# The last group's output in token order, four right-side buffers, and parts spread over fourteen steps

## The chip, the cores and the metric

One Trainium2 chip; the kernel runs on one of its cores. The metric is device time in microseconds (us), the median of several executions. Names of engines: PE is TensorE's matmul, PEld its weight load, DVE is VectorE, ACT is ScalarE, POOL is GpSimd, SP is SyncE, which only issues DMAs. SPq and ACTq are the DMA issues on the queues of SP and ACT.

## What is computed

An attention with decay (retention) over 4 batches, 8 heads, 768 positions and 64 columns gives 3072 tokens of 512 columns. Two feed-forward layers follow, each 512 to 2048 to 512, everything in 32-bit floats:

```python
x = attention(q, k, v)                  # 3072 x 512
h = x @ w_in;  x = (h * cos(h)) @ w_out
h = x @ w2_in
g = np.where(h >= 1, h, np.where(h <= -1, 0.0, (h + 1) ** 2 / 4))
out = g @ w2_out                        # 3072 x 512
```

## The kernel before

**Number format.** Each matmul operand is split into a high part (fp32r, a rounding copy made by ScalarE, line 139) and a low part (the difference, made by GpSimd at line 142 or 1002, or by VectorE). A product of two operands takes three matmuls: high by high, low by high, high by low. One matmul has 128 x 128 stationary values and 512 moving columns.

**Order of the work.** The attention fills the first steps. The first layer has 96 `steps`: a step is one chunk of 128 hidden columns for one of six blocks of 512 tokens. Steps 0 to 47 take the first eight chunks for all blocks, steps 48 to 95 the other eight, and add the first half's sums when a block is finished. Step i runs `first(i)` (12 matmuls, line 681), `second(i - 3)` (12 matmuls, line 768) and `act(i)`: rounding copy on ScalarE (line 719), high and low part of the step before, `evacuate` (line 779) of a finished block's four accumulators, cosine, then `fill` (a list of extra work), then one advance of the `Conveyor`, which converts the second layer's weights. Engines work each through their own instructions in this program order.

**Weights of the second layer.** `Convert` decodes pairs of chunks; `combine` forms four sums of half chunks (line 267), and `part` writes high and low parts of each piece and queues stores to `wp` (sent by SP, line 296). A pair has four pieces, three of 512 and one of 256 columns. The last pair is started in steps 83 and 84 and its pieces are made in step 89.

**Second layer (`Products`).** It pairs blocks (three pairs p = 0, 1, 2) and pairs of hidden chunks (8), which gives 24 groups g. Each group uses a scheme with seven products in place of eight, named 11, t1, 21, t2, 22, t3, t4. The right sides are the tokens (sums and differences of quarters), the left sides are weights. Group g has seven sections; in each, PE does one product of group g (6 matmuls, line 961) and one output of group g - 1 (6 matmuls, line 977), which VectorE adds to one of four running sums (`acc`, line 1035). Between them ScalarE and VectorE evaluate the ramp and square (lines 1005, 1006, 1009, 1012, 1109, 1105, 1015) and `high` and `low` make the operands of the outputs. Operands live in a ring of eight pairs of buffers (`pairs`).

The order in which a right side's seven parts are made is `TURN`: t2, t1, t3, t4, 11, 21, 22. For p = 0 `make(0)` and `make(1)` do that in the fills of steps 80 to 95. `make(0)` places its differences in buffers that later take high parts, so that each high copy overwrites what the part made just before it was read from:

```python
at = dict(zip(TURN[:4] + ("12",), TURN[1:4] + ("11", "21")))
x.update({q: place(at[q], "h", F32) for q in at})
```

For p = 1 and 2 `remake` does it in the groups of the pair before, one `tick` per section: 11, 21, 22 of the first half, then t2, t1, t3, t4, then the same seven of the second half (11', ...). Each part's high copy goes to `xhi` (two buffers), and two stores to DRAM (`xb`, line 925) follow, the high part's in the next section.

**The end.** Group 24 has no products, only group 23's outputs. VectorE does `t4`'s difference and low parts there. The last four sums are added in halves (line 1031), and `final` transposes each with 8 PE transposes (line 1077), copies the results out of PSUM (lines 1084, 1086) into token order, and stores 256 KB per token tile (line 1091).

Of the kernel before, what the change touches and what calls it, by code (L numbers as in the profile page):

```python
# [11 lines left out]
F32 = mybir.dt.float32  # L12
# [28 lines left out]
def tile_retention_mlp_mlp(  # L41
# [42 lines left out]
        for m, j, a in [(0, j, a) for j in range(NH, NF) for a in range(2)] + order2[:READY]  # L84
# [5 lines left out]
             for g in range(NH)] for a in range(2)]  # L90

# [81 lines left out]
    class Convert:  # L173
# [72 lines left out]
        def combine(self):  # L246
# [22 lines left out]
        def part(self, n):  # L269

            to = wp_d[self.a][self.j // 2][n]
# [8 lines left out]
            stores.append((to[:, 0, :], hi[:, :wide[n]].bitcast(F32)))  # L280
# [508 lines left out]
    class Products:  # L789
# [7 lines left out]
        def __init__(self):  # L797
            self.w, self.x, self.f, self.g = {}, {}, {}, {}
            self.spare, self.ready = [], []
            self.done, self.turned, self.out = {}, {}, {}  # L800
            self.rows, self.finals = [], []
# [3 lines left out]
            self.pairs = [("wi", n) for n in range(NH + NP + 1, NF)] + [("g", 0)] * 3  # L805
# [17 lines left out]
        def load(self, a, g, n):  # L823
# [7 lines left out]
            self.w[a, g, n] = slot, t  # L831

# [72 lines left out]
        def remake(self, p):  # L905
# [12 lines left out]
            def parts(c, q):  # L918
                hi = self.tmp.tile([P, TB], F32R, tag="xhi", name="xhi", bufs=2)
# [16 lines left out]
            return fs  # L936

# [80 lines left out]
        def add(self):  # L1018
            if not self.pending:
                return  # L1020
            g, q, y, fine = self.pending.pop(0)
# [7 lines left out]
            elif fine and final:  # L1029
                for e in range(2):  # L1030
                    nc.vector.tensor_tensor(out=a[:, e, :], in0=y[:, e, :], in1=a[:, e, :], op=ALU.add)
                self.finals.append((a, p, h, n))
                return
            else:
                nc.vector.tensor_tensor(out=a, in0=y, in1=a, op=ALU.add)  # L1035
# [31 lines left out]
        def final(self):  # L1067

            if not self.finals:
                return  # L1070
            a, p, h, n = self.finals.pop(0)
            z = self.z[2 * self.nz:2 * self.nz + 2]
            self.nz = 1 - self.nz
            z = [t[:, o:o + 2 * P] for t in z for o in (0, 2 * P)]
            for e in range(2):
                for i in range(NP):
                    nc.tensor.transpose(z[i][:, e * P:(e + 1) * P], a[:, e, i * P:(i + 1) * P], self.eye)
            if h == 0:
                self.out[n] = self.big()
            for i in range(NP):  # L1080
                o = self.out[n][:, i, :].rearrange("p (k c b) -> p c k b", k=4, c=4)[:, 2 * h:2 * h + 2]
                src = z[i].rearrange("p (e k b) -> p e k b", k=4, e=2)
                if i < 2:
                    nc.vector.tensor_copy(out=o, in_=src)
                else:
                    nc.scalar.activation(out=o, in_=src, func=AF.Copy)
            if h == 0:
                return
            for i in range(NP):
                t0 = (i * NC + 2 * p + n) * C  # L1090
                (nc.sync, nc.scalar)[i // 2].dma_start(out=out[t0:t0 + C, :], in_=self.out[n][:, i, :])

        def group(self, g, banks, ends):


            live, prev = g < self.NG, g - 1
            fine = prev == self.NG - 1
# [21 lines left out]
            def outputs(q, to, begin):  # L1119
# [3 lines left out]
                if prev >= 0:  # L1123
                    self.output(prev, q, to, begin)
                    self.pending.append((prev, q, to, fine))

            def done(n, m):
                if prev >= 0:
                    self.release(1, prev, n)
                    self.load(1, g, m)  # L1130

            o = self.old
            if live:
                a = bank(banks[0])
                self.product(g, "11", a, True)
# [4 lines left out]
            if live:  # L1140
                s1 = copy(a)
            if o:
# [3 lines left out]
                fast = nc.vector if fine else nc.gpsimd  # L1146
                fast.tensor_tensor(out=t4, in0=o["r21"], in1=self.f[prev, "t2"], op=ALU.subtract)
# [4 lines left out]
            if prev >= 0:  # L1152
                self.load(1, g, 0)

            if live:
                b = bank(banks[1])
                self.product(g, "t1", b, True)
# [7 lines left out]
            if live:  # L1165
                s5 = copy(b)
# [3 lines left out]
            if live:  # L1170
                tick()

            if live:
                c = bank(banks[2])
                self.product(g, "21", c, True)
                self.release(0, g, 0)
                self.load(0, g + 1, 1)
            self.add()
            if o:
                self.low(prev, "21")  # L1180
                self.low(prev, "t4", fast)
            if live:
                plus(c, c, s1)
                r11 = self.take(g, "11")
                self.ramp(r11, c)
# [3 lines left out]
            if live:  # L1189
                tick()  # L1190

            if live:
                self.product(g, "t2", a, False)
                self.release(0, g, 1)
                self.load(0, g + 1, 2)
            self.add()
            if live:
                s6 = copy(a)
                self.square(r11)
                self.larger(r11, r11, c)  # L1200
            outputs("22", y1, False)
            self.turn_out("21")
            if live:
                tick()

            if live:
                self.product(g, "22", b, False)
            self.add()
            if live:
                self.high(g, "11")  # L1210
# [488 lines left out]
```

## Time and profile before

| what | value |
|---|---|
| median of 3 runs | 1102.06 us (1097.68 to 1102.06) |
| the profiled execution: time | 1098.7 us |
| the profiled execution: span | 1096.9 us |
| PE busy | 1070.3 us |
| DVE, POOL, ACT busy | 804.3, 614.4, 603.7 us |
| DMA | 279.95 MB, 255 GB/s |

The span runs from the first to the last instruction of the profiled execution; its time is 1.8 us more. Matmuls are pipelined: of several in a row each shows about 0.39 us, and one begins every 0.227 us. A row of the timeline has start, duration, engine, line and operation, output and inputs, shape and count, and in brackets the engine's idle time before it with what ended it.

### The profile page before, as it was taken

The numbers are of one execution on the slowest core, as the hardware profiler recorded it, in microseconds if no ns is written. First come the engines' busy times: TensorE is split into PE (matmuls) and PEld (weight loads), VectorE is DVE, ScalarE is ACT, GpSimd is POOL, SyncE is SP. The second block draws the span as 40 slices with busy tenths as digits, with TensorE's granted clock in tenths as the row PEclk, the third lists the DMA queues.
The fourth block names the chain that finished last, engine by engine and source line by source line (L and its number), as shares of the span: only waits on it lengthen the run. The fifth ranks groups of instructions, "written<-read, shape, count | busy, mean of one in ns | idle before, by whom it ended". The sixth has DMA issues, their size and how long they took to land.

```text
span 1096.9 us, 17870 instructions
## 1 busy us (share of the span) xinstructions
PE 1070.3 (98%) x6286; PEld 868.2 (79%) x6286; DVE 804.3 (73%) x1101; ACT 603.7 (55%) x1078; POOL 614.4 (56%) x525
## 2 busy tenths in 40 slices
PE   8999999999999999999999999999999899999996
PEld 5677788888888888888887888787888688888884
DVE  5778878877667447869774578678887677978776
ACT  3454334433355445546465567677677676666662
POOL 3834212221146368878998248787368785564642
PEclk9999999999999999999999999999999999999999
DMA  9588389895667599989978677889598899576542
GB/s 340 173 295 277 110 241 307 271 322 172 214 212 260 194 298 323 337 305 310 302 253 273 245 238 254 296 289 388 170 293 259 268 320 360 175 249 204 179 143 87
DMA packets 139897, 279.95 MB, mean 255 GB/s; under 512 B 15520, under 2 KB 41760, under 8 KB 139808
## 3 DMA queue, kind: packets, MB, share of 16 engines
q1 hardware_dynamic: 124256, 250.49, 69.3%
q10 hardware_dynamic: 15552, 28.32, 7.5%
q8 instruction: 50, 0.82, 0.3%
q14 instruction: 39, 0.32, 0.1%
HBM read 195.39 MB, written 83.36 MB: 254 GB/s over the span
## 4 chain that ended last, share of the span: by engine, by line
PE 83%; DMA 6%; DVE 5%; POOL 2%; issue 2%; ACT 1%; SPq 0%; DVEq 0%; ACTq 0%; POOLq 0%
PE b L768 22%; PE b L681 21%; PE b L961 17%; PE y L977 17%; PE b L580 2%; PE b L487 1%; DVE big L1043 1%; DMA xb2t20h<-xhi 1%; DMA qk<-in_qk 1%; PE b L498 1%; DMA xb1t20h<-xhi 1%; DMA wp<-whi 1%; DMA xl<-xTl 1%; DMA xb1t21h<-xhi 1%; DMA xb2t21h<-xhi 1%
## 5 line engine op out<-in xcount | busy, mean ns | idle before, releaser
L719 ACT ACTIVATE r<-b 128x512 int32<-128x512 f32 x96 | 57.1, 595 | 188.6 <-PE b L681 140.0
L724 DVE SCALAR_TENSOR_TENSOR r<-b,r 128x512 f32<-128x512 f32 x96 | 66.0, 688 | 114.7 <-ACT r L719 110.6
L230 POOL TENSOR_TENSOR cf<-cf,cs 128x512 int32<-128x512 int32 x42 | 54.4, 1295 | 147.1 <-DVE cf L221 98.3
L1035 DVE TENSOR_TENSOR xh<-y,xh 128x1024 f32<-128x1024 f32 x88 | 107.0, 1220 | 27.0 <-PE y L977 25.9
L1113 POOL TENSOR_TENSOR ft<-r,f 128x512 f32<-128x512 f32 x24 | 31.2, 1299 | 123.2 <-PE y L977 92.0
L768 PE MATMUL b<-gh,wo 128*128 128x512 f32 x384 | 98.2, 390 | 1.6 <-DVE o L779 1.6
L977 PE MATMUL y<-wi,wo 128*128 128x512 f32 x360 | 93.8, 395 | 5.5 <-ACT xhi L139 3.0
L681 PE MATMUL b<-xh,wi 128*128 128x512 f32 x384 | 94.8, 389 | 0.0
L1035 DVE TENSOR_TENSOR xl<-y,xl 128x1024 f32<-128x1024 f32 x64 | 77.9, 1216 | 13.7 <-PE y L977 13.7
L961 PE MATMUL b<-wih,wi 128*128 128x512 f32 x320 | 87.1, 390 | 0.4 <-DVE b L1105 0.4
L977 PE MATMUL y<-gh,wo 128*128 128x512 f32 x272 | 85.1, 395 | 2.3 <-DVE xh L1035 2.3
L768 PEld LDWEIGHTS b<-gh,wo 128*128 128x128 f32 x384 | 71.8, 188 | 17.5 <-ACT r L730 2.0
L977 PEld LDWEIGHTS y<-wi,wo 128*128 128x128 f32 x360 | 67.7, 190 | 22.2 <-ACT xhi L139 4.2
L681 PEld LDWEIGHTS b<-xh,wi 128*128 128x128 f32 x384 | 72.1, 188 | 14.9
L737 ACT ACTIVATE gh<-b 128x512 fp32r<-128x512 f32 x96 | 57.1, 595 | 38.0 <-DVE b L733 37.5
L768 PE MATMUL b<-gh,woh 128*128 128x512 f32 x192 | 77.4, 408 | 0.5 <-ACT woh L139 0.5
L681 PE MATMUL b<-xh,wih 128*128 128x512 f32 x192 | 75.4, 395 | 1.6 <-ACT wih L139 0.9
L681 PE MATMUL b<-xh,wil 128*128 128x512 f32 x192 | 74.3, 390 | 0.0
L768 PE MATMUL b<-gh,wol 128*128 128x512 f32 x192 | 74.0, 391 | 0.0
L1002 POOL TENSOR_TENSOR gl<-ft,gh 128x512 fp32r<-128x512 f32 x56 | 71.7, 1298 | 1.3 <-ACT gh L139 1.3
L961 PEld LDWEIGHTS b<-wih,wi 128*128 128x128 f32 x320 | 59.9, 188 | 13.6 <-DVE b L1105 1.3
L733 DVE TENSOR_TENSOR b<-b,r 128x512 f32<-128x512 f32 x96 | 66.6, 693 | 2.6 <-ACT r L730 0.3
(173 smaller groups left out, 2770.3 us busy)
## 6 DMA issues: line engine op xcount, KB each, us to landing
wi<-wp SPq DMA_DIRECT2D x66, 512.0 KB, 4.7
wo<-wp SPq DMA_DIRECT2D x66, 512.0 KB, 5.1
raw<-in_w SPq DMA_DIRECT2D x64, 512.0 KB, 6.0
wp<-whi SPq DMA_DIRECT2D x48, 256.0 KB, 3.9
wp<-s SPq DMA_DIRECT2D x32, 256.0 KB, 3.7
w<-cf ACTq DMA_DIRECT2D x26, 256.0 KB, 5.4
xTh<-xh ACTq DMA_DIRECT2D x24, 256.0 KB, 5.7
xTl<-xl ACTq DMA_DIRECT2D x24, 256.0 KB, 5.9
```

Source lines behind the costliest of these rows:

```text
L230: nc.gpsimd.tensor_tensor(out=f, in0=f, in1=self.s, op=ALU.add)
L681: nc.tensor.matmul(out=h, lhsT=w[:, c * P:(c + 1) * P], rhs=x[:, c, :], start=(i == 0), stop=(i == len(terms) - 1),)
L719: nc.scalar.activation(out=self.r.bitcast(I32), in_=self.h, func=AF.Identity, scale=INV_2PI, bias=0.25)
L724: nc.vector.scalar_tensor_tensor(out=self.r, in0=self.h, scalar=INV_2PI, in1=self.r.bitcast(I32), op0=ALU.mult, op1=ALU.subtract,)
L733: nc.vector.tensor_tensor(out=self.h, in0=self.h, in1=self.r, op=ALU.mult)
L737: nc.scalar.activation(out=self.gh, in_=self.h, func=AF.Copy)
L768: nc.tensor.matmul(out=acc[k, b][e], lhsT=w[:, s], rhs=g, start=(begin and i == 0), stop=(last and i == 2),)
L961: nc.tensor.matmul(out=to, lhsT=w[:, c * P:(c + 1) * P], rhs=x, start=begin and n == 0, stop=n == len(terms) - 1, skip_group_check=not begin,)
L977: nc.tensor.matmul(out=to[:, e, :], lhsT=w[:, e * P:(e + 1) * P], rhs=a, start=begin and m == 0, stop=m == 2, skip_group_check=not begin,)
L1002: eng.tensor_tensor(out=lo, in0=self.f.pop((g, q)), in1=hi.bitcast(F32), op=ALU.subtract)
L1035: nc.vector.tensor_tensor(out=a, in0=y, in1=a, op=ALU.add)
L1113: nc.gpsimd.tensor_tensor(out=o, in0=x, in1=z, op=ALU.subtract)
```

## The change

Three things are changed.

1. Group 23 makes no differences t1, t2, t3, t4; it keeps the four plain operands 11, 12, 21, 22, and there is no group 24. `close` runs behind it. It transposes the four sums of the groups up to 22 (`turned`, 8 PE transposes each time), copies them into token order on ScalarE, and multiplies the plain operands with plain weights (`load_plain`) so that the product is in token order already (`tile`: two halves, four tiles, 6 matmuls each). VectorE adds a tile's product to the transposed sum, and the tile is stored at once, by SP and ACT in turn. For the plain weights the last weight pair gets a fifth piece of 256 columns, `wx`.
2. `xhi` has four buffers, as two tiles of two halves. The second tile takes the place of one pair of the operand ring, which has seven pairs after.
3. `make(0)` puts its eleven fills at steps 80 + 0, 1, 3, 4, 5, 6, 8, 9, 10, 12, 13 in place of 80 + 0 to 8 with the last three in one step.

```diff
             if self.a:
                 a12, a21 = a21, a12
                 self.pieces[0] = [(a11, 0), (a12, h)]
+                if self.j == NF - 1:
+                    self.pieces[4] = [(a21, 0)]
...
                 self.part(3)
                 self.part(0)
+                if 4 in self.pieces:
+                    self.part(4)
...
-            self.pairs = [("wi", n) for n in range(NH + NP + 1, NF)] + [("g", 0)] * 3
+            self.pairs = [("wi", n) for n in range(NH + NP + 1, NF - 1)] + [("g", 0)] * 3
+            self.highs, self.turns = [], 1
...
+        def load_plain(self, n):
+            slot = self.slots[1].pop(0)
+            t = wpool[1].tile([P, 2, TB], F32R, tag=f"{slot[0]}{slot[1]}", name=f"{slot[0]}{slot[1]}")
+            h = TB // 2
+            first, *_, fourth = wp_d[1][NH - 1]
+            for o, d in ((0, first[:, :, n * h:(n + 1) * h]), (h, fourth if n else wx_d)):
+                nc.sync.dma_start(out=t[:, :, o:o + h].bitcast(F32), in_=d)
+            self.plain[n] = t[:, 0, :], t[:, 1, :]
...
             def parts(c, q):
-                hi = self.tmp.tile([P, TB], F32R, tag="xhi", name="xhi", bufs=2)
+                hi = self.next_high()
...
+        def next_high(self):
+            if not self.highs:
+                n = self.turns = 1 - self.turns
+                pool, tag = (wpool[1], f"wi{NF - 1}") if n else (self.tmp, "xhi")
+                t = pool.tile([P, 2, TB], F32R, tag=tag, name="xhi")
+                self.highs = [t[:, 0, :], t[:, 1, :]]
+            return self.highs.pop(0)
...
+        def close(self, banks):
...
+            def turned(n, i):
+                z = self.ps.tile([P, 2, TB], F32, tag=f"y{(g + 1 + i // 2) % 2}", name="z")
+                for m in range(2):
+                    for c in range(NP):
+                        a = self.acc["12"[c // 2] + "12"[n]]
+                        nc.tensor.transpose(
+                            z[:, m, c * P:(c + 1) * P], a[:, c % 2, (i + m) * P:(i + m + 1) * P], self.eye
+                        )
...
+            def half(n, i, k):
+                if k == 0:
+                    ys[i] = bank(banks[(2, 1, 3, 0)[i]])
+                (wh, wl), (gh, gl) = self.plain[k], self.g[g, names[n][k]][1]
+                for m, (a, w) in enumerate(((gh, wh), (gh, wl), (gl, wh))):
+                    nc.tensor.matmul(
+                        out=ys[i], lhsT=a[:, i * P:(i + 1) * P], rhs=w,
+                        start=k == m == 0, stop=k == 1 and m == 2,
+                    )
...
+                    t0 = (i * NC + 2 * p + n) * C
+                    (nc.sync, nc.scalar)[i % 2].dma_start(out=out[t0:t0 + C, :], in_=o)
+
+            self.add()
+            r21, h21 = self.old["r21"], self.old["h21"]
+            self.square(r21)
+            self.larger(h21, r21, h21)
+            self.f[g, "21"] = h21
+            turned(1, 0)
+            self.high(g, "21")
+            self.low(g, "21", nc.vector)
+            tile(1, 0, 1)
+            turned(1, 2)
+            tile(1, 2)
+            turned(0, 0)
+            tile(1, 3)
+            tile(0, 0)
+            turned(0, 2)
+            for i in range(1, NP):
+                tile(0, i)
...
+            if end:
+                self.f[g, "12"] = r12
+                self.high(g, "12")
+            else:
                 t1 = self.take(g, "t1")
                 minus(t1, r12, r11)
...
-                    for n, f in enumerate(fast.make(0)):
-                        ready.setdefault(i + min(n, NH), []).append(f)
+                    for n, f in zip((0, 1, 3, 4, 5, 6, 8, 9, 10, 12, 13), fast.make(0)):
+                        ready.setdefault(i + n, []).append(f)
                     for n, f in zip((0, 2, 3, 3, 3, 4, 4, 5, 5, 6, 7), fast.make(1, stage)):
                         ready.setdefault(i + NH + n, []).append(f)
```

## Rows read from the trace of the kernel before

**Rows 1.** The page: busy time; costliest groups (count | busy us, mean ns | idle before)

```profile
PE 1070.3 (98%) x6286; PEld 868.2 (79%) x6286; DVE 804.3 (73%) x1101; ACT 603.7 (55%) x1078; POOL 614.4 (56%) x525
...
L733 DVE TENSOR_TENSOR b<-b,r 128x512 f32<-128x512 f32 x96 | 66.6, 693 | 2.6 <-ACT r L730 0.3
```

**Rows 2.** What PE waited for: us in total, times, longest

```profile
PE y L977 <- ACT xhi L139: 3.0, 1, 3.0
...
PE y L977 <- POOL wi L1002: 1.7, 3, 0.7
...
PE b L768 <- DVE o L779: 1.6, 1, 1.6
```

**Rows 3.** Timeline of PE at the end

```profile
1069.76 2.88 PE L977 MATMUL y<-wi,wo 128*128 128x512 f32 x12
...
1077.19 0.71 PE L977 MATMUL y<-gh,wo 128*128 128x512 f32 x2 [2.30 <-DVE xh L1035]
```

**Rows 4.** A window: us, busy us and instructions by engine, granted clock, DMA share, GB/s

```profile
1077.20:1083.00 5.80, 5.80 (x18) 4.57 (x19) 3.98 (x5) 0.00 (x0) 0.47 (x1) 0.71 0.01 3
```

**Rows 5.** The chain that ended last: start, us, what

```profile
847.44 8.86 DMA xb2t20h<-xhi
...
1064.48 1.36 PE y L977 x6
...
1085.44 1.08 PE b L1077 x8
```

**Rows 6.** Timeline of ACT in groups 23 and 24

```profile
1056.18 0.63 ACT L139 ACTIVATE wi<-ft 128x512 fp32r<-128x512 f32 x1
...
1071.76 0.63 ACT L1009 ACTIVATE f<-f 128x512 f32<-128x512 f32 x1
...
1091.94 0.82 ACTq L1091 DMA_DIRECT2D out<-big  x2
```

**Rows 7.** DMA issues of the last 17 us: KB each, median us to landing

```profile
out<-big ACTq DMA_DIRECT2D x4, 256.0 KB, 3.0
```

**Rows 8.** What ACT waited for, the `xhi` copies: us, times, longest

```profile
ACT xhi L139 <- DMA xb2t20h<-xhi: 5.8, 1, 5.8
...
ACT xhi L139 <- DMA xb1t20h<-xhi: 2.9, 1, 2.9
...
ACT xhi L139 <- DMA xb1t21h<-xhi: 2.6, 1, 2.6
...
ACT xhi L139 <- DMA xb2t21h<-xhi: 2.2, 1, 2.2
```

**Rows 9.** Timeline of PE behind two of these waits

```profile
700.98 0.70 PE L977 MATMUL y<-wi,wo 128*128 128x512 f32 x2
...
702.43 1.19 PE L977 MATMUL y<-wi,wo 128*128 128x512 f32 x4 [0.74 <-POOL wi L1002]
...
859.49 1.16 PE L977 MATMUL y<-wi,wo 128*128 128x512 f32 x2 [3.03 <-ACT xhi L139]
...
860.90 2.08 PE L977 MATMUL y<-wi,wo 128*128 128x512 f32 x4 [0.26 <-POOL wi L1002]
```

**Rows 10.** Timeline of ACT, the last instruction before the longest of them

```profile
849.93 0.63 ACT L1006 ACTIVATE r<-r 128x512 f32<-128x512 f32 x1
```

**Rows 11.** Timeline of PE in step 91

```profile
580.48 2.43 PE L768 MATMUL b<-gh,wo 128*128 128x512 f32 x8 [1.61 <-DVE o L779]
```

**Rows 12.** Timeline of ACT, steps 87 and 90

```profile
567.50 0.63 ACT L139 ACTIVATE woh<-wih 128x512 fp32r<-128x512 f32 x1 [1.42 <-POOL wol L142]
...
577.84 0.58 ACT L719 ACTIVATE r<-b 128x512 int32<-128x512 f32 x1
```

**Rows 13.** Timeline of POOL, steps 87 and 88

```profile
568.67 1.31 POOL L142 TENSOR_TENSOR wol<-wih,woh 128x512 fp32r<-128x512 f32 x1
...
572.87 2.56 POOL L142 TENSOR_TENSOR s<-s,whi 128x512 fp32r<-128x512 f32 x2
...
577.32 2.54 POOL L142 TENSOR_TENSOR wil<-wil,wih 128x512 fp32r<-128x512 f32 x2
```

More of the change, by code (lines that the diff above doesn't have):

```diff
@@ L799, in __init__ @@
             self.spare, self.ready = [], []
-            self.done, self.turned, self.out = {}, {}, {}
-            self.rows, self.finals = [], []
+            self.done, self.turned, self.plain = {}, {}, {}
+            self.rows = []
             self.queue = [[], []]
@@ L1028, in add @@
                 nc.vector.tensor_copy(out=a, in_=y)
[L1029 to L1033, printed above, removed]
             else:
@@ L1152, in group @@
             if prev >= 0:
[L1153 to L1157, printed above, removed]
+                load(0)
+            b = bank(banks[1])
+            self.product(g, "t1", b, True)
             self.add()
@@ L1169, in group @@
             self.turn_out("22")
[L1170 to L1177, printed above, removed]
+            tick()
+            c = bank(banks[2])
+            self.product(g, "21", c, True)
+            self.release(0, g, 0)
+            self.load(0, g + 1, 1)
             self.add()
@@ L1180, in group @@
                 self.low(prev, "21")
[L1181 to L1185, printed above, removed]
+                self.low(prev, "t4")
+            plus(c, c, s1)
+            r11 = self.take(g, "11")
+            self.ramp(r11, c)
             outputs("t2", y0, False)
@@ L1188, in group @@
             done(1, 1)
[L1189 to L1195, printed above, removed]
+            tick()
+            self.product(g, "t2", a, False)
+            self.release(0, g, 1)
+            self.load(0, g + 1, 2)
             self.add()
[L1197 to L1200, printed above, removed]
+            s6 = copy(a)
@@ L1201, in group @@
+            self.square(r11)
+            self.larger(r11, r11, c)
             outputs("22", y1, False)
             self.turn_out("21")
[L1203 to L1207, printed above, removed]
+            tick()
+            self.product(g, "22", b, False)
             self.add()
-            if live:
-                self.high(g, "11")
-                plus(b, b, s6)
-                r12 = r()
-                self.ramp(r12, b)
+            self.high(g, "11")
@@ L1214, in group @@
+            plus(b, b, s6)
+            r12 = r()
+            self.ramp(r12, b)
             outputs("t3", y0, False)
-            self.final()
             done(2, 2)
-            if live:
-                tick()
-            if live:
-                self.product(g, "t3", a, False)
-                self.release(0, g, 2)
-                self.load(0, g + 1, 3)
-            self.add()
-            if live:
-                d = bank(banks[3])
-                plus(d, a, s5)
-                self.square(r12)
-                self.larger(r12, r12, b)
+            tick()
@@ L1230, in group @@
+            self.product(g, "t3", a, False)
+            self.release(0, g, 2)
+            self.load(0, g + 1, 3)
+            self.add()
+            d = bank(banks[3])
+            plus(d, a, s5)
+            self.square(r12)
+            self.larger(r12, r12, b)
+            if end:
+                self.f[g, "12"] = r12
+                self.high(g, "12")
+            else:
                 t1 = self.take(g, "t1")
                 minus(t1, r12, r11)
-                self.low(g, "11")
-                r22 = r()
@@ L1249, in group @@
+            self.release(0, g, 3)
+            self.load(0, g + 2, 0)
             self.add()
-            if live:
-                self.square(r22)
-                self.larger(d, r22, d)
+            self.square(r22)
+            self.larger(d, r22, d)
+            if end:
+                self.f[g, "22"] = d
+                self.low(g, "12")
+                self.high(g, "22")
+                self.low(g, "22", nc.vector)
+            else:
                 self.high(g, "t1")
@@ L1280, in run @@
             banks = (4, 6, 7, 5)
-            for g in range(self.NG + 1):
+            for g in range(self.NG):
                 if g == 0:
```

109 lines of the change are left out of this document (51 added, 58 removed).

## The prediction

> **What bounds the kernel now.** I read the page first: TensorE is busy for 98% of the span [rows 1]. So only three things can move the end: fewer or cheaper matmuls, TensorE's idle time, and what lies before its first and after its last instruction. Second, the list of what TensorE waited for. Three of its entries lie where this change works [rows 2]: 3.0 us on an `xhi` copy of ScalarE, 1.7 us on GpSimd's low parts just behind such copies, and 1.6 us on an evacuation (line 779). Third, the timeline of the end. Group 23's last six matmuls (the outputs `t4` of group 22) are the first half of the x12 piece at 1069.76, so they end at 1069.76 + 1.36 = 1071.12. What follows until 1096.9, 25.8 us, is group 24 alone: outputs, waits, transposes, copies, stores. TensorE waits 2.30 us there [rows 3], and then gets a granted clock of 0.71 in that stretch [rows 4], which is partly its lower level of 1.2 GHz.
>
> **Part 1: the last group.** Before, the end is a chain of small steps: 42 matmuls, and 32 transposes that each need a finished sum. After, the products of group 23 are put in token order: 2 halves x 4 token tiles x 2 operands x 3 terms = 48 matmuls of 512 columns. The 32 transposes remain, but read sums of groups up to 22, so they can run while ScalarE and VectorE still make the last operands. Six matmuls take 1.36 us, so 48 take 10.9; eight transposes take 1.08 [rows 5], four sets 4.3 at most. TensorE is through 15.2 us after 1071.12, at 1086.3, if it never waits.
>
> Does it wait? The operands come one after another. The latest is `21`: its square ends at 1071.76 + 0.63 = 1072.4 before [rows 6]. After, ScalarE does a copy for `12` and one for `22` ahead of it (0.6 each) and VectorE's low part of `22` and a sum of 1.2 stand between, which I put at 1.8 together: 1074.2. Maximum 0.7, the two copies out of PSUM that ScalarE does first, the high part 0.6 and the low part 0.7 give 1076.6. The matmuls that need `21` come after two sets of transposes and 18 matmuls (6.3 us), a third set and the tile (1,3): from 1078 on. Slack 1.5 us, so I take no stall. The new weight loads are issued in steps 1 and 3 of group 23, more than 8 us before use.
>
> Behind the last matmul: 0.2 us to drain, 0.7 for one 128x512 add of VectorE [rows 1], then one store. Before, 1096.9 - 1091.94 = 5.0 us pass between the last issue and the end [rows 6], with four stores of 256 KB at once; such a store lands after 3.0 us [rows 7]. After, the last one has few beside it. Between 3.0 and 5.0 I take 4.0: 1086.3 + 0.9 + 4.0 = 1091.2, a gain of 5.7 us; 4.7 and 6.7 at the bounds.
>
> The Trainium skill ("DMA: Bandwidth & Descriptors", Anatomy of one DMA) has a fixed cost of about 2.0 us plus the bytes at 436 GB/s, which is an estimate of 2.6 us for 256 KB; by it the term would be 7.1 us. The row's 3.0 us agrees nearly, but not the 5.0 to the end, so I stay with rows.
>
> **Part 2: four right-side buffers.** With two, the copy for `t3` needs the store of `t2`'s high part, issued two steps (2 x 2.72 us) earlier. ScalarE waited four times for such a store: 5.8, 2.9, 2.6 and 2.2 us [rows 8]. What TensorE lost: in the 5.8 us case 3.03 + 0.26 idle, and six matmuls spread over 1.16 + 2.08 us instead of 1.52, together 5.0 us; in the 2.9 us case two matmuls start at 700.98 and the next four at 702.43 where 0.45 us would do, 1.0, and about 0.3 before them [rows 9]. The other two show the same picture at smaller size, so 5.0 + 1.3 + 1.1 + 0.6 = 8.0 us in all is the most that this can give.
>
> The four buffers are two tiles of two halves, and a tile is taken anew only when both halves are read. Counting parts from `11`, the pairs are (11, 21), (22, t2), (t1, t3), (t4, 11'), and so on. So `t3` of the first half no longer waits, but `t4`, one step later, waits for `22` and `t2`: the stall is late by a step, not gone. The store of `t2` landed at 847.44 + 8.86 = 856.3 [rows 5]. ScalarE was ready for `t3` at 849.93 + 0.63 = 850.6 [rows 10], so it is ready for `t4` some 2.6 us later, at 853.2, and waits 3.1 us in place of 5.8. In the 2.9 us case 0.3 is left, and in the second halves `t3` waits for `22`, which was issued a step before `t2`: nothing. The shortened wait no longer holds up the operands of `11`, but still those of `t1` and `t2` of the next group; carrying 3.1 us through VectorE, GpSimd and the slack of a step leaves TensorE some 2 us late. So 5.0 - 2.0 + 3.0 = 6.0 us gained; 3.0 if the wait costs what it did, 8.0 if it costs nothing.
>
> Two buffers come out of the ring of operand pairs (eight become seven). The tightest use is `t4`: its copy starts at 1056.18 [rows 6], and the buffer's former reader, the last output of the group before, ended at 1071.12 - 19.04 = 1052.08. Slack 4 us: no cost.
>
> **Part 3: the parts of the first right side.** Steps 80 to 95 are the last two blocks. Before, `t2`, `t1`, `t3`, `t4` are made in steps 84 to 87 and three more in step 88; after, in 85, 86, 88, 89, 90, 92, 93. The pile in 88 looks like the cause of the 1.61 us that TensorE waits at 580.48 [rows 11], since ScalarE runs late there: the rounding of step 90 starts at 577.84 [rows 12], and the evacuation, which frees the banks for block 5, follows it on VectorE. But look at who holds ScalarE. Each part's high copy overwrites the buffer that its predecessor's low part, on GpSimd, still reads: `t4` waited 1.42 us for the low part of `t3` [rows 12]. GpSimd has no gap there. Behind `t4`'s low part (568.67, 1.31) it works off step 87's weight conversion (four sums, then low parts from 572.87, done at 577.32) and only then the parts of step 88 [rows 13]. After, `t4`'s low part is not in front, so that conversion is done at 577.32 - 1.25 = 576.1, then comes the low part of `t3` (step 88): 577.3. And `t4`'s high copy (step 89) must wait for that. Before, nothing in step 89 waited. Then 0.55 for the copy, 1.96 for the five copies of the weight conversion and 0.4 for the sixth, which the new right-half weights add: step 90's rounding starts at 580.2 instead of 577.84, 2.4 us later. TensorE waits 4.0 us in place of 1.6. The matmuls after a wait are slow: eight in 2.43 us here where 1.98 would do, six in 1.7 us more than usual after the wait of 3.03 [rows 9, 11]; between these I take 0.6 more than now. So part 3 costs 3.0 us. Bounds: 4.3 (GpSimd later by one more low part of 1.3), and a gain of 1.61 + 0.45 = 2.1 if the whole stall goes.
>
> The Trainium skill ("TensorE: Matmul & The Clock Gate", Architectural detail) says that ScalarE's queue is strictly first in, first out; if a waiting copy could be passed by, the sum would be better by these 3.0 us. The 1.42 us wait agrees with the rule: no ScalarE instruction starts inside it.
>
> The three parts that go to steps 92 and 93 meet engines with gaps; first use at 605 or later, so nothing. The extra weight piece adds one GpSimd op of 256 columns and two stores, counted above or hidden.
>
> **Sum.** -5.7 - 6.0 + 3.0 = -8.7 us on the profiled execution: 1098.7 - 8.7 = 1090.0. The median of the runs, 1102.06, lies 3.4 higher (runs from 1097.68), so against it 1093.4. I say 1091.
>
> **Rivals.**
> (a) The spread does what it seems made for: `t3`'s low part gets in ahead, step 90 is on time, the stall goes. For it: the pile in 88 is real (three copies). Against: the order of GpSimd's queue. -5.7 - 6.0 - 2.1 = -13.8: 1084.9. Chance 0.2.
> (b) The wait for `t2`'s store only changes place and costs as before: -5.7 - 3.0 + 3.0: 1093.0. For it: pairs of halves; against: `11`'s operands get past. 0.13.
> (c) The new end stalls: ScalarE's in-order queue holds an output store that waits for VectorE, and the copies behind it, so transposes and tiles wait; part 1 gives 1 us: 1094.7. Decides from 4 us of waits on; I found 1.5 us of slack. 0.12.
> (d) Slower: seven pairs instead of eight make each group wait. It needs `t4`'s buffer to be read 4 us longer than now; from 0.4 us in each of 22 groups the 8.7 us are gone, at 0.8 us it is 1098.7 + 8.9 = 1107.6. Against: no ScalarE wait for TensorE on such a copy shows now. 0.06.
> The forecast has the remaining 0.49.
>
> Half a per cent, 5.5 us, is about what a measurement tells from no change. Forecast (but for its weak edge), (a) and half of (b) lie beyond it: 0.74 faster; (c), the other half and the edge 0.19 same; (d) and a little of (c) 0.07 slower. The range goes from just below (a), 1083.5, to (c) read against the median, 1098.5; the forecast's own bounds are 1087 to 1095.
>
> **What would show it.** Right: no idle above 0.5 us on TensorE between the last product and the last tile, and an end some 20 us after that product; no ScalarE wait on `t3`, one of about 3 us on the first `t4` of the third pair of blocks; a TensorE wait on line 779 of about 4 us. Wrong: that wait gone (a), a new one on a pair's high copy in every group (d), or a TensorE wait between the tiles (c).

## The result and the profile after

The changed kernel takes 1089.01 us (median of 5 runs, 1086.05 to 1090.17); the kernel before, run beside it, 1102.06 us (5 runs, 1096.38 to 1102.4). The ratio is 0.9896, with a 95% interval of 0.9866 to 0.9926: 13 us less by the medians and 11.4 by the ratio, which goes by the means (8.1 to 14.7). The profiled execution took 1089.38 us, with a span of 1087.6.

The profiled pair differs by only 9.3 us in span. The rest lies where nothing was changed: the first matmul of step 80 starts at 516.15 us in the profile of before and at 519.62 in that of after, and in a second profile of the kernel before it starts at 521.97. So the 3.5 us of this pair lie within what two executions of one program differ by, and I compare stretches from step 80 on.

The page of the changed kernel, part 1 (answers to [rows 1]):

```profile
PE 1069.6 (98%) x6292; PEld 869.8 (80%) x6292; DVE 793.3 (73%) x1087; ACT 603.2 (55%) x1076; POOL 609.7 (56%) x522
```

TensorE's work is the same to 0.7 us; only idle time and the end can have moved. What PE waited for in the changed kernel, from the first product to the end of the last one (us in total, times, longest):

```profile
PE b L986 <- DVE b L1166: 0.4, 2, 0.2
```

That is the whole list. The 3.0 us for the `xhi` copy and the 1.7 us for GpSimd behind it [rows 2] are gone. Here is why; ScalarE's `xhi` copies of the third pair's first half, `t2` to `t4`, in the changed kernel (timeline; 850.38 is `t1`, 854.22 is `t3`):

```profile
848.55 0.62 ACT L141 ACTIVATE xhi<-big 128x512 fp32r<-128x512 f32 x1
...
854.22 0.62 ACT L141 ACTIVATE xhi<-big 128x512 fp32r<-128x512 f32 x1
...
857.16 0.63 ACT L141 ACTIVATE xhi<-big 128x512 fp32r<-128x512 f32 x1 [0.35 <-DMA xb2t20h<-xhi]
```

The timeline of SP has the store of `t2`'s high part, and the view of the DMA issues has its time to landing (last number, us):

```profile
849.77 1.00 SPq L942 DMA_DIRECT2D xb2t20h<-xhi  x1
```

```profile
xb2t20h<-xhi SPq DMA_DIRECT2D x1, 256.0 KB, 7.3
```

`t3` waits for nothing, `t4` waits 0.35 us where I had put 3.1. The same copy and its landing in the kernel before:

```profile
844.80 0.62 ACT L139 ACTIVATE xhi<-big 128x512 fp32r<-128x512 f32 x1
```

```profile
xb2t20h<-xhi SPq DMA_DIRECT2D x1, 256.0 KB, 8.9
```

Steps 87 to 91 show the new cost. ScalarE in the changed kernel: `t3`'s high copy (step 88), `t4`'s (step 89), and the rounding of step 90 (answers to [rows 12]):

```profile
574.79 0.63 ACT L141 ACTIVATE woh<-woh 128x512 fp32r<-128x512 f32 x1 [1.96 <-POOL s L271]
...
576.67 0.63 ACT L736 ACTIVATE r<-r 128x512 f32<-128x512 f32 x1 [0.27 <-DVE r L730]
580.06 0.63 ACT L141 ACTIVATE woh<-wih 128x512 fp32r<-128x512 f32 x1 [2.76 <-POOL wol L144]
...
582.86 0.57 ACT L725 ACTIVATE r<-b 128x512 int32<-128x512 f32 x1
```

GpSimd at the same time (answers to [rows 13]):

```profile
574.29 2.54 POOL L144 TENSOR_TENSOR s<-s,whi 128x512 fp32r<-128x512 f32 x2
576.79 1.98 POOL L144 TENSOR_TENSOR f<-f,whi 128x256 fp32r<-128x256 f32 x2
578.73 1.29 POOL L144 TENSOR_TENSOR wol<-woh,woh 128x512 fp32r<-128x512 f32 x1
```

`t3`'s low part (578.73) stands behind the low parts of step 87's weight conversion (574.29, 576.79) and ends at 580.02; `t4`'s high copy starts at 580.06. TensorE then (answers to [rows 11]):

```profile
585.50 3.20 PE L774 MATMUL b<-gh,wo 128*128 128x512 f32 x8 [3.17 <-DVE o L785]
588.50 1.65 PE L774 MATMUL b<-gl,wo 128*128 128x512 f32 x4
```

A window of the changed kernel from 585.50 on, whose seventh figure behind the colon (ahead of the DMA share) is the granted clock:

```profile
585.50:591.00 5.50, 5.50 (x17) 4.12 (x18) 4.25 (x7) 2.24 (x4) 5.50 (x7) 0.69 1.04 382
```

The wait is 3.17 us in place of 1.61, and the twelve matmuls behind it take 1.3 us more than in [rows 11] (3.20 in place of 2.43, then 1.65 for the last four, which took 1.08 before), at a granted clock of 0.69: part of them at the lower level, 1.2 GHz.

The end, from the chain that ended last (start, us, what; answers to [rows 3, 5]):

```profile
1067.81 1.36 PE y L1002 x6
1069.17 0.87 PE z L1100 x8
1070.05 2.74 PE b L1118 x12
1072.79 0.88 PE z L1100 x8
1073.67 1.38 PE b L1118 x6
1075.05 0.87 PE z L1100 x8
1075.92 2.75 PE b L1118 x12
1078.67 0.87 PE z L1100 x8
1079.55 4.11 PE b L1118 x18
...
1083.75 0.69 DVE big L1129
```

Each piece begins where the last one ends: TensorE never waits. From its last output of group 22 (1069.17) to the end of the span, 18.4 us pass; they were 25.8. Windows over these tiles show full clock, where [rows 4] had 0.71:

```profile
1069.17:1075.05 5.88, 5.88 (x37) 5.04 (x35) 4.40 (x7) 3.81 (x7) 0.00 (x0) 1.00 0.01 3
1075.05:1083.70 8.65, 8.59 (x46) 6.99 (x44) 3.94 (x6) 3.15 (x6) 0.00 (x0) 1.00 0.49 182
```

The last store is issued when the add ends, 1084.44; the timeline of ACT and the DMA issues of the last 4 us have it (answers to [rows 6, 7]):

```profile
1084.47 0.34 ACTq L1135 DMA_DIRECT2D out<-big  x1
```

```profile
out<-big ACTq DMA_DIRECT2D x1, 256.0 KB, 2.0
```

So the store lands 2.0 us after its issue, at about 1086.5, and the span ends 1.1 us later.

### The profile page after: what moved, and what is told of

It is laid out like the page before. It is cut to its first block, busy times and chain, and to the rows that moved or that the text cites. A ratio compares the mean times of both kernels' runs of the same rounds, so it can differ in the third digit from the quotient of the medians.

```text
span 1087.6 us, 17859 instructions
## 1 busy us (share of the span) xinstructions
PE 1069.6 (98%) x6292; PEld 869.8 (80%) x6292; DVE 793.3 (73%) x1087; ACT 603.2 (55%) x1076; POOL 609.7 (56%) x522
## 4 chain that ended last, share of the span: by engine, by line
PE 84%; DMA 6%; DVE 5%; POOL 2%; issue 1%; ACT 1%; SPq 0%; ACTq 0%; DVEq 0%; POOLq 0%
PE b L774 20%; PE b L986 20%; PE b L687 20%; PE y L1002 19%; PE b L586 1%; DMA xTl<-xl 1%; DMA w<-cf 1%; PE b L1118 1%; DVE big L1063 1%; PE b L493 1%; PE b L476 1%; DMA wp<-whi 1%; DMA xh<-xTh 1%; DMA raw<-in_w 1%; DMA qk<-in_qk 1%
## 5 line engine op out<-in xcount | busy, mean ns | idle before, releaser
L1002 PE MATMUL y<-wi,wo 128*128 128x512 f32 x276 | 70.2, 390 | 0.1
L1002 PE MATMUL y<-wo,wo 128*128 128x512 f32 x276 | 70.0, 389 | 0.0
L736 ACT ACTIVATE r<-r 128x512 f32<-128x512 f32 x96 | 60.6, 631 | 14.6 <-DVE r L730 14.6
```

The source lines that it names most:

```text
L736: nc.scalar.activation(out=self.r, in_=self.r, func=AF.Sin, scale=TWO_PI, bias=HALF_PI)
L1002: nc.tensor.matmul(out=to[:, e, :], lhsT=w[:, e * P:(e + 1) * P], rhs=a, start=begin and m == 0, stop=m == 2, skip_group_check=not begin,)
```

## The experiments

The theory has three parts. The end gains what its TensorE time and one store allow. The buffers gain what the `xhi` waits cost TensorE, less a wait that stays on `t4`. The spread loses because `t4`'s high copy must wait for `t3`'s low part, which GpSimd reaches only behind a weight conversion. The rivals: the spread helps, and another thing delays step 90 (the new fifth weight piece, `wx`); the buffers' gain comes from something else, or seven pairs take it back; the parts depend on each other.

**Each part alone.** `tail_only` is the changed kernel without parts 2 and 3:

```diff
-                hi = self.next_high()
+                hi = self.tmp.tile([P, TB], F32R, tag="xhi", name="xhi", bufs=2)
...
-                    for n, f in zip((0, 1, 3, 4, 5, 6, 8, 9, 10, 12, 13), fast.make(0)):
-                        ready.setdefault(i + n, []).append(f)
+                    for n, f in enumerate(fast.make(0)):
+                        ready.setdefault(i + min(n, NH), []).append(f)
```

(with the eighth pair put back into `pairs`).

> The kernel before with part 1 alone (close, plain weights, the wx piece; two xhi buffers, eight pairs, old placement of the parts). Theory: the stretch from TensorE's last output of group 22 to the end of the span is about 18.4 us as in the changed kernel, in place of 25.8, so some 7.4 us less and a ratio near 0.993; the waits on xhi copies stay (about 3 us on TensorE), and TensorE's wait on the evacuation in step 91 stays at 1.6 us, or 2.0 if the sixth weight copy delays ScalarE by 0.4. Rival (the wx piece, not the order of the parts, made that wait longer in the changed kernel): it is 3 us here too.

Measured: 0.9919 of the kernel before, 0.9903 to 0.9934; 1092.2 us. Counted from the last product of the groups, the end takes 19.90 us, against 27.14 in the profile of before: 7.2 us, beyond my bounds for this term (4.7 to 6.7). Part of that is the clock: the old end of 27.1 us has a fall of it [rows 4], and two profiles below (`spread_only`, `xhi_only`) have the old end without the fall, in 25.83 and 26.00 us. Against these the new end gains 5.9 and 6.1 us.

`xhi_only` is the kernel before with `next_high` and seven pairs:

```diff
-            self.pairs = [("wi", n) for n in range(NH + NP + 1, NF)] + [("g", 0)] * 3
+            self.pairs = [("wi", n) for n in range(NH + NP + 1, NF - 1)] + [("g", 0)] * 3
+            self.highs, self.turns = [], 1
...
-                hi = self.tmp.tile([P, TB], F32R, tag="xhi", name="xhi", bufs=2)
+                hi = self.next_high()
```

> The kernel before with part 2 alone (four xhi buffers as two tiles of two halves, seven operand pairs). Theory: no TensorE wait on an xhi copy or on a low part behind one; ScalarE waits under 1 us for the store of t2 at t4; 8 us less than the profile of before, ratio near 0.993. Rival (the 5.0 us loss on the third pair of blocks was chance in that one execution): only 3 to 4 us less, ratio 0.997. Rival (the seventh pair costs): a ScalarE wait on a pair's high copy in every group, ratio 1 or more.

Measured: 0.9932, 0.9911 to 0.9953; 1093.03 us. From the first product to the end of the last one the groups take 456.43 us, against 464.33 and 463.44 in two profiles of the kernel before: 7.0 to 7.9 us. What ScalarE waited for (us, times, longest) still has `t4`'s copy:

```profile
ACT xhi L139 <- DMA xb2t20h<-xhi: 2.3, 1, 2.3
ACT xhi L139 <- DMA xb1t20h<-xhi: 1.2, 1, 1.2
```

and the timeline of PE shows what the 2.3 us cost:

```profile
857.99 0.61 PE L970 MATMUL b<-xl,wi 128*128 128x512 f32 x2
859.31 1.63 PE L986 MATMUL y<-wi,wo 128*128 128x512 f32 x6 [0.70 <-ACT gh L139]
```

0.70 us, and 0.1 more in the six matmuls. Both are more than I expected of this run: under 1 us on ScalarE, and no wait of TensorE. Of the twelve profiles this is the only one in which a wait of `t4` for that store still reached TensorE.

`spread_only` is the kernel before with the eleven fills at their new steps and nothing else, so without the fifth weight piece:

```diff
-                    for n, f in enumerate(fast.make(0)):
-                        ready.setdefault(i + min(n, NH), []).append(f)
+                    for n, f in zip((0, 1, 3, 4, 5, 6, 8, 9, 10, 12, 13), fast.make(0)):
+                        ready.setdefault(i + n, []).append(f)
```

> The kernel before with part 3 alone (the eleven fills of the first right side over fourteen steps). Theory (t4's high copy stands behind t3's low part, which GpSimd reaches only after the weight conversion): TensorE waits 2.8 to 3.2 us on the evacuation in step 91 in place of 1.6, ScalarE waits over 2 us for GpSimd ahead of t4's copy, 2 to 3 us slower, ratio 1.002 to 1.003. Rival (the wx piece did it): the wait is 1.6 us or less, and the time the same or 2 us better.

Measured: 1.002, 1.0002 to 1.0037; 1102.85 us, 2.2 us more by the ratio (0.2 to 4.1). ScalarE's timeline and PE's show the predicted pair:

```profile
581.14 0.63 ACT L139 ACTIVATE woh<-wih 128x512 fp32r<-128x512 f32 x1 [2.79 <-POOL wol L142]
```

```profile
586.27 2.43 PE L768 MATMUL b<-gh,wo 128*128 128x512 f32 x8 [3.16 <-DVE o L779]
588.54 1.09 PE L768 MATMUL b<-gl,wo 128*128 128x512 f32 x4
```

The wait on TensorE is that of the changed kernel, without `wx`; in `tail_only`, which has `wx` and the old steps, it is 1.32 us. The rival that blames `wx` falls. Here the matmuls behind the wait are not slower than in [rows 11]; I come back to that.

**The changed kernel without the spread.** `no_spread` undoes part 3 in the changed kernel by the second half of `tail_only`'s diff.

> The changed kernel without part 3 (old placement of the parts; parts 1 and 2 kept). Theory: TensorE's wait on the evacuation in step 91 is back at 1.6 to 2.0 us, and the time is 2 to 3 us less than the changed kernel's: ratio to before 0.986 to 0.988 beside 0.9896 for the whole change. Rival (spreading the parts helps or does nothing): ratio 0.990 or more, and the wait stays at 3.2 us.

Measured: 0.9877, 0.9851 to 0.9903; 1087.83 us. The wait is back to 1.84 us. But the matmuls behind it are slow this time (timeline of PE, then a window with the granted clock):

```profile
584.75 2.92 PE L774 MATMUL b<-gh,wo 128*128 128x512 f32 x8 [1.84 <-DVE o L785]
587.47 1.91 PE L774 MATMUL b<-gl,wo 128*128 128x512 f32 x4
```

```profile
584.75:590.25 5.50, 5.50 (x16) 3.90 (x17) 4.24 (x7) 2.23 (x4) 5.50 (x7) 0.69 0.92 292
```

By the times alone its interval overlaps that of the changed kernel, so how large part 3's loss is beside the other two isn't told by this run.

**Do the parts add up?** By the ratios the three parts alone give -8.9, -7.5 and +2.2 us, together -14.2; the whole change gives -11.4, and -12.2 in `after_again` below. The intervals of the parts, some 2 us each to either side, don't tell these sums apart, so the rival that the parts depend on each other by 2 to 3 us is neither shown nor ruled out.

**The order on GpSimd's queue.** If the order is what costs, `t3`'s part put one step earlier, in front of step 87's conversion, must take the wait away. `t3_early` does only that to the changed kernel:

```diff
-                    for n, f in zip((0, 1, 3, 4, 5, 6, 8, 9, 10, 12, 13), fast.make(0)):
+                    for n, f in zip((0, 1, 3, 4, 5, 6, 7, 9, 10, 12, 13), fast.make(0)):
```

> The changed kernel with one part moved by one step: t3 in step 87 in place of 88 (fills at 80 + 0, 1, 3, 4, 5, 6, 7, 9, 10, 12, 13). Theory: t3's low part is then ahead of step 87's weight conversion on GpSimd, so t4's copy in step 89 waits for nothing; ScalarE loses its 2.8 us wait there and TensorE's wait falls from 3.2 us to under 1. Rival (it is the number of parts or the wx piece in these steps, not the order of t3 and the conversion): the wait stays near 3 us, since the parts and the pieces are as many as before.

Measured: 0.9864, 0.9837 to 0.989; 1086.0 us. GpSimd's timeline, then ScalarE's, then PE's:

```profile
570.62 1.29 POOL L144 TENSOR_TENSOR wol<-woh,woh 128x512 fp32r<-128x512 f32 x1
571.88 1.43 POOL L271 TENSOR_TENSOR s<-f 128x256 f32<-128x256 f32 x2
```

```profile
576.40 0.62 ACT L141 ACTIVATE woh<-wih 128x512 fp32r<-128x512 f32 x1
...
579.66 0.58 ACT L725 ACTIVATE r<-b 128x512 int32<-128x512 f32 x1
```

```profile
582.31 2.43 PE L774 MATMUL b<-gh,wo 128*128 128x512 f32 x8 [0.39 <-DVE o L785]
```

`t3`'s low part now stands ahead of the conversion's four sums; `t4`'s copy waits for nothing; step 90's rounding starts at 579.66 in place of 582.86; TensorE waits 0.39 us. From that rounding to the end of TensorE's wait it is 2.65 us here and 2.64 in the changed kernel and in the kernel before [rows 11, 12]: the wait follows the rounding to a hundredth.

`late_three` keeps the first four parts at their old steps (84 to 87) and leaves only the last three late:

```diff
-                    for n, f in zip((0, 1, 3, 4, 5, 6, 8, 9, 10, 12, 13), fast.make(0)):
+                    for n, f in zip((0, 1, 2, 3, 4, 5, 6, 7, 10, 12, 13), fast.make(0)):
```

> The changed kernel with only the last three parts of the first right side spread (fills at 80 + 0, 1, 2, 3, 4, 5, 6, 7, 10, 12, 13). Theory: t4's high copy goes back ahead of the weight conversion of step 87 on GpSimd, and the three copies of step 88 no longer stand in ScalarE's queue, so the rounding of step 90 starts some 1.6 us earlier than before and TensorE's wait on the evacuation falls from 1.6 (before) and 3.2 us (changed) to under 0.5: 4 to 5 us less than the changed kernel, ratio to before 0.984 to 0.987. Rival (ScalarE is late for another reason, the run-up of steps 82 to 87): the wait stays above 1.5 us.

Measured: 0.9874, 0.9848 to 0.99; 1086.91 us, some 2 us less than the changed kernel, where I had put 4 to 5. TensorE's wait is 0.86 us, less than in the kernel before but more than I had put down for this run (under 0.5). ScalarE's timeline shows what is left: the sixth, small copy of the weight conversion in step 89 waits for a store.

```profile
582.12 0.42 ACT L141 ACTIVATE whi<-f 128x256 fp32r<-128x256 f32 x1 [1.12 <-DMA wp<-whi]
```

So both readings of step 88 had something: with the pile of three parts out of it the wait is 0.9 us, where two profiles of before have 1.6 and 2.1, and `t3` behind the conversion puts it at 3.2.

**Seven pairs.** `ring7` is the kernel before with only the shorter ring:

```diff
-            self.pairs = [("wi", n) for n in range(NH + NP + 1, NF)] + [("g", 0)] * 3
+            self.pairs = [("wi", n) for n in range(NH + NP + 1, NF - 1)] + [("g", 0)] * 3
```

> The kernel before with seven operand pairs in place of eight and nothing else. Theory: the same time within half a per cent, no new ScalarE wait on an operand's high copy in the groups (slack 4 us). Rival: at 0.4 us in each of 22 groups some 9 us more, ratio 1.008.

Measured: 0.9987, 0.9967 to 1.0008; 1099.28 us. Seven pairs cost at most 0.9 us by the interval; rival (d) falls.

**The kernel before once more**, one execution, for the spread between profiles of one program:

> The kernel before once more, for a second profile. If the long wait for the store of t2 on the third pair of blocks (5.8 us on ScalarE, 3.03 us on TensorE) belongs to the kernel, it is there again within 1 us; if it was chance in one execution, ScalarE waits 2 to 3 us there as at the other three places. The first 80 steps, where the changed kernel's profile is 3.5 us later than the first profile of before, show how far two executions of one program differ there.

1104.19 us; wait on the evacuation 2.14 us, the wait for `t2`'s store 5.5 us, the groups 463.44 us, the end 27.13 us: all within 0.9 us of the first profile.

**The changed kernel and its best version side by side:**

> The changed kernel once more, beside t3_early_again on one chip. 0.990 of the kernel before; TensorE waits about 3 us on the evacuation in step 91, and nothing above 0.5 us elsewhere between the first product and the last tile.

> The changed kernel with only t3's part moved from step 88 to step 87. If the order on GpSimd's queue is what costs (my theory), the wait in step 91 is below 1 us and the time is 3 to 4 us less than that of after_again: 0.986 to 0.987 of the kernel before. If the difference of the first run was chance between executions (rival), both give 0.990 within 1 us of each other.

Measured: `after_again` 0.9889, 0.9873 to 0.9906 (1089.51 us, 1088.34 to 1090.72); `t3_early_again` 0.9864, 0.9842 to 0.9886 (1085.43 us, 1084.74 to 1089.54), 4.1 us less by the medians. One of its four runs lies at 1089.54, and the two intervals overlap, so these times alone make the 4 us likely, not sure. Taken with the first runs of both kernels, nine of ten of `t3_early` lie between 1084.7 and 1086.9 us, and eight of nine of the changed kernel between 1088.3 and 1090.8. The two profiles agree with it; PE's waits in `after_again` and in `t3_early_again`:

```profile
PE b L774 <- DVE o L785: 3.4, 1, 3.4
```

```profile
PE b L774 <- DVE o L785: 1.2, 1, 1.2
```

From step 91's first matmul to the first product the one takes 32.66 us and the other 29.04: 3.6 us. Of these 2.2 are the shorter wait and 1.3 the slow clock behind it in `after_again`, which does not come with every such wait (last section). The 1.2 us is a little above what I expected; the sixth copy of step 89 waited 0.61 us for a store here. The version with `t3` in step 87 is the fastest that I ran.

All profiles, in numbers worked out from the timelines (us; "rest of block" is from step 91's first matmul to the first product, "groups" from there to the end of the last product, "end" from that to the end of the span, where a matmul is taken to end 0.23 us after its start; the clock is that granted in the 5.5 us from the end of the wait on):

| kernel | `t4`'s copy waits for GpSimd | TensorE waits on the evacuation | clock behind it | rest of block | groups | end |
|---|---|---|---|---|---|---|
| before | 1.42 | 1.61 | 1.00 | 29.43 | 464.33 | 27.14 |
| before_again | 2.67 | 2.14 | 1.00 | 29.99 | 463.44 | 27.13 |
| ring7 | 2.7 | 1.65 | 1.00 | 29.48 | 461.48 | 27.13 |
| tail_only | 1.4 | 1.32 | 1.00 | 29.20 | 462.83 | 19.90 |
| xhi_only | 2.7 | 1.82 | 1.00 | 29.66 | 456.43 | 26.00 |
| spread_only | 2.79 | 3.16 | 1.00 | 31.00 | 465.64 | 25.83 |
| no_spread | 2.67 | 1.84 | 0.69 | 31.29 | 456.25 | 19.93 |
| after | 2.76 | 3.17 | 0.69 | 32.28 | 455.90 | 19.96 |
| after_again | 2.83 | 3.39 | 0.69 | 32.66 | 455.65 | 19.91 |
| late_three | 1.41 | 0.86 | 1.00 | 28.69 | 457.94 | 19.91 |
| t3_early | none | 0.39 | 1.00 | 28.22 | 456.82 | 19.92 |
| t3_early_again | none | 1.20 | 1.00 | 29.04 | 456.25 | 19.94 |

In the kernels with the old steps the copy that waits is in step 87 and has two steps to catch up before step 90; with the new steps it is in step 89 and has none. So a wait of 2.7 to 2.8 us on ScalarE goes with 1.7 to 2.1 us on TensorE in the one place and with 3.2 to 3.4 in the other.

The store that `t3` (two buffers) or `t4` (four) waits for, `t2`'s of the third pair's first half, in all twelve profiles (us; worked out from the timelines of ACT and SP and the landing of this one issue):

| kernel | buffers | SP issues it after the copy's end | issue to landing | copy's end to landing | ScalarE waits |
|---|---|---|---|---|---|
| before | 2 | 2.0 | 8.9 | 10.9 | 5.8 |
| before_again | 2 | 2.0 | 8.6 | 10.6 | 5.5 |
| spread_only | 2 | 1.9 | 8.3 | 10.2 | 5.1 |
| ring7 | 2 | 1.3 | 7.2 | 8.5 | 3.4 |
| tail_only | 2 | 0.6 | 7.8 | 8.4 | 3.3 |
| xhi_only | 4 | 2.3 | 7.6 | 9.9 | 2.3 |
| no_spread | 4 | 1.8 | 7.1 | 8.9 | 1.3 |
| t3_early | 4 | 0.6 | 7.6 | 8.2 | 0.6 |
| t3_early_again | 4 | 0.6 | 7.5 | 8.1 | 0.5 |
| late_three | 4 | 0.6 | 7.3 | 7.9 | 0.4 |
| after | 4 | 0.6 | 7.3 | 7.9 | 0.35 |
| after_again | 4 | 0.6 | 6.9 | 7.5 | none |

The wait is the fifth column less 5.1 us with two buffers and less 7.6 us with four, to 0.1 us in every row.

The third column has a cause in the traces. In SP's order four loads `big<-yT` and three weight loads stand ahead of this store, and the first of the four starts when the store `xb2220l` has landed. SP's timeline in the kernel before and in the changed one:

```profile
843.33 2.59 SPq L860 DMA_DIRECT2D big<-yT  x4
```

```profile
845.82 1.74 SPq L877 DMA_DIRECT2D big<-yT  x4
```

That is 2.1 us ahead of the end of `t2`'s copy before and 3.4 after. In the six profiles where it is 3.1 us or more, SP issues `t2`'s store 0.6 us behind the copy; in the six where it is 2.1 to 2.7 us, 1.3 to 2.3 us behind. So the late landing of one store delays the issue of the next.

## Why the prediction was right, and where it was off

The direction and the range held (1089.01 in 1083.5 to 1098.5), and 1091 was 2.0 us too much. The terms, cut where the table of all profiles cuts them: the end -7.2 us (-7.4 by the forecast's cut, which said -5.7), the groups -8.4 (forecast -6.0), the rest of the block +2.9 (forecast +3.0). They sum to -12.8 (-12.76), near the medians' -13.05 (the ratio gives -11.4); the profiled pair itself shows 3.5 less, which lies before step 80. The agreement of 1091 with the result is better than its terms, and partly luck: two of them were 1.7 and 2.4 us too small, and 1091 was chosen between the 1090.0 of the profiled execution and the 1093.4 of the median. The sum taken from the median, 1093.4, is 4.4 us too much.

**Part 1: right in mechanism, the sum off by 1.7 us.** The matmuls took what I said (48 in 10.98 us, against 10.9) without a wait. The 7.4 us are counted, as the forecast's 5.7, against an end with a fallen clock; against the two old ends without the fall the term is 1.1 to 1.3 us smaller. Two terms beside them were mis-sized. Four sets of transposes took 3.49 us, not 4.3. The chain of before has two full sets of eight, and I took the dearer one of [rows 5]; the set just ahead of it in the same view has the price that came true:

```profile
1083.17 0.87 PE b L1077 x8
```

And the last store: from the end of the last add to the end of the span it is 3.16 us, where I took 4.0 between 3.0 and 5.0. The landing of 3.0 us [rows 7] was the nearer row. The 5.0 us had other stores in it, and I read the row of [rows 6] wrongly: it holds two issues, and 1091.94 is the start of the first. The second, 4.5 us ahead of the end:

```profile
1092.38 0.39 ACTq L1091 DMA_DIRECT2D out<-big  x1
```

The transposes and the store together are 1.65 of the 1.7 us.

`21`'s low part was ready at 1074.33, and its first matmul comes nine into the twelve from 1075.92, at 1078.0: a slack of 3.6 us, where I had 1.5. The forecast's "from 1078 on" left out terms that it names: with the third set and the tile (1,3) behind the 6.3 us its own numbers give 1071.12 + 6.3 + 1.1 + 1.4 = 1079.9. And its 1076.6 leaves only 0.4 us for two copies out of PSUM, which took 1.07 us. Rival (c) falls: what ScalarE waits for at the end is TensorE's transposes, 2.4 us at most, and no store holds it.

By the Trainium skill ("DMA: Bandwidth & Descriptors", Anatomy of one DMA) the store was an estimate of 2.6 us, and the term 7.1. The section describes the path of GpSimd's DMAs, while these stores are issued by SP and ACT; the trace has 2.0 us for such a store alone and 7.4 for the term.

**Part 2: the step that failed is the 3.1 us wait on `t4` and the 2 us that it leaves on TensorE.** That `t4` waits in `t3`'s place with 2.6 us more to spare held: 2.5 us by the second table (7.6 less 5.1). But I took the landing of `t2`'s store from one profile as if it were fixed. In that profile it came 10.9 us after the copy, the latest of twelve; in the changed kernel 7.9 us. So 5.8 - 2.5 - 3.0 = 0.3 us of wait, and 0.35 was measured. Half of the 3.0 is SP, which issued the store 2.0 us after the copy before and 0.6 after it now; the other half is the way from issue to landing. Both vary with two buffers as they do with four (0.6 to 2.0 and 0.6 to 2.3 us to the issue, 7.2 to 8.9 and 6.9 to 7.6 us to landing), so the buffers are not shown to be what brought the store in sooner; what is shown is the 2.5 us. SP's part goes with the landing of an earlier store (behind the second table). And what TensorE loses for a wait on `t4` was too high as well: 0.8 us at 2.3 us of wait (`xhi_only`), nothing at 1.3 (`no_spread`). Rival (b) falls with it, and `ring7` rules out that the shorter ring took back more than 0.9 us.

The gain of 8.4 us is that of the profiled pair, with the late landing in it. Over the profiles the groups take 461.48 to 465.64 us with two buffers (five, mean 463.5) and 455.65 to 457.94 with four (seven, mean 456.5): 7.1 us, between my 6.0 and the 8.0 that I called the most. `late_three`'s 457.94 has 1.4 us of waits for loaded weights in it; no other profile has more than 0.12.

**Part 3: right, in mechanism and in size, but the size is made of two things.** ScalarE's wait came where it was put, for `t3`'s low part behind the conversion (2.76 us), and the rounding of step 90 is late by it. The wait of TensorE grew by 1.6 us, not by 2.4, and the slow matmuls behind it by 1.3, not 0.6. The wait repeats in every kernel that has `t3` in step 88 (3.16, 3.17, 3.39 us). The slow matmuls do not: `spread_only` has the wait without them, and its loss by the ratio is 2.2 us. The wait was put too high because GpSimd was done with the conversion sooner than I said: at 578.73, which is 575.3 when the 3.5 us from before step 80 are taken off, where I had 576.1. From there to the rounding it took 4.1 us, as forecast. Rival (a), the spread as a help, falls for these steps: only with `t3` one step earlier does the wait go, and the time that I gave for (a), 1084.9, is then nearly reached, 1085.43 and 1086.0.

That a waiting ScalarE lets nothing pass is told by the trace: between 577.30, the end of the instruction at 576.67, and 580.06 it starts nothing, though the product that step 90's rounding reads was done at 576.9. The rule of the Trainium skill ("TensorE: Matmul & The Clock Gate", Architectural detail), strictly first in, first out, agrees.

## What to carry to other kernels

When work is spread over more steps, write down for each moved piece what its buffer's last reader is, on which engine that reader stands, and behind what: here one part moved by one step changed a wait from 3.2 to 0.4 us (3.4 to 1.2 in the second pair), and the page's shares of busy time don't tell it (TensorE 98% in both kernels). Price a wait for a store by the slack that a change adds, and take the landing as a range from several profiles, since here it moved the wait by up to 2.5 us for the same code around it. For the end of a kernel, count what TensorE must still do plus one add and one store, and price the store by its landing when it is alone.

## What was not expected of the hardware

**The clock behind a short wait is not the same each time.** In step 91 TensorE does the same work before and after the wait in these kernels. Behind waits of 1.84 us in `no_spread` and of 3.17 and 3.39 us in `after` and `after_again` the granted clock was 0.69 over the next 5.5 us, in all three; behind 2.14 us in `before_again` and 3.16 us in `spread_only` it stayed at 1.00. The window of `spread_only`:

```profile
586.27:591.77 5.50, 5.50 (x23) 4.01 (x24) 4.24 (x7) 2.24 (x4) 5.50 (x7) 1.00 1.05 393
```

So the length of the wait does not decide it here, and a fall cost 1.2 to 1.3 us on the next twelve matmuls. Even at a granted 1.00 the first eight matmuls behind the wait take 2.43 or 2.44 us in place of 1.98, in each of the nine profiles without a fall.

The old end does the same. Behind its wait of 2.3 us the clock of the next 5.8 us was 0.71 in `before` [rows 4], `before_again` and `ring7`, and 1.00 in `xhi_only` and `spread_only`:

```profile
1071.44:1077.24 5.80, 5.75 (x28) 4.58 (x29) 4.54 (x7) 0.23 (x1) 0.48 (x1) 1.00 0.01 3
```

```profile
1084.32:1090.12 5.80, 5.77 (x28) 4.58 (x29) 4.55 (x7) 0.25 (x1) 0.48 (x1) 1.00 0.01 3
```

There the end is 1.1 to 1.3 us shorter (first table). What decides was not tried.

**A store alone is quick.** A store of 256 KB lands in 2.0 us at the end of the changed kernel, against 3.0 with others beside it [rows 7] and 6.9 to 8.9 us in the middle of the groups (second table).
